# Row-paired transposes for the token-major rows and the attention output, and half 0's memory scores placed behind the third group of row pairs

## Chip, core and metric

The kernel runs on one NeuronCore of a Trainium2 chip. The metric is the device time of one launch in microseconds (us). The core's engines are named as the profile names them: PE is the matrix engine (PEld its weight loads), DVE the vector engine, ACT the scalar engine, POOL the GpSimd engine, SP the engine that issues most transfers.

## What is computed

Two layers are applied twice to x (2048 tokens of 448 elements, bf16): A, attention with a recurrent memory, and B, a gated feed-forward layer. Each takes the layer-normed x, and its result is added to x. The reference, cut to the parts that matter (H = 16 heads of 256, M = 8 memory rows, segments of 32 tokens, F = 1792):

```python
def _A_ref(x, mem0, Wq, Wk, Wv, Wo, seg_len):
    ...
    mask = (idx[:, None] < M) | (idx[:, None] >= idx[None, :])
    mem = mem0
    for s in range(n_seg):                      # 64 segments, one after another
        h = jnp.concatenate([mem, xs], axis=1)  # 8 memory rows and 32 tokens
        q, k, v = (einsum('btd,dhe->bhte', h, W) for W in (Wq, Wk, Wv))
        scores = jnp.einsum('bhqe,bhke->bhqk', q, k) * scale
        p = _softmax(jnp.where(mask, scores, -1e9))
        o = jnp.einsum('bhqk,bhke->bhqe', p, v)
        o = jnp.einsum('bhte,hed->btd', o, Wo)
        mem = o[:, :M, :]                       # the next segment's memory
        outs.append(o[:, M:, :])

def _B_ref(x, W_gate, W_up, W_down):
    gate = x @ W_gate
    h = gate * (gate > 0) * (x @ W_up)
    return h @ W_down

x = x + _A_ref(_layernorm(x), ...); x = x + _B_ref(_layernorm(x), ...)
x = x + _A_ref(_layernorm(x), ...); x = x + _B_ref(_layernorm(x), ...)
```

## The kernel before

**Weights are fused first.** A prologue builds, for each head, Wq Wk^T (`A_sb`, `A3`, `A3z`) and Wv Wo (`B_sb`). Attention then needs only h itself: queries are h times the fused matrix, keys and values are the rows h.

**Two chains in one step.** Layer A runs twice over the sequence, and the second run (chain 1) follows the first (chain 0) four segments later. `step(g, ff)` (lines 575 to 810) does segment g of chain 0 and segment g - 4 of chain 1 together; there are 69 steps, of which those with g from 4 to 63 have both chains. The 80 columns of a step are 40 rows of each chain. Every second step (odd g) also carries a `Feed` object `ff`: the feed-forward layer for a block of 64 tokens of each chain. These are called feed steps here, the others plain steps.

**The order on PE is written out by hand.** All matmuls and transposes go through `mm` and `tr` (lines 80 to 84), and `in_order` (lines 72 to 78) chains each to the one before. The order on DVE and ACT isn't fixed in this way: the framework that compiles the kernel orders their instructions by its own reckoning and adds all semaphores.

**PSUM banks.** A PSUM tile takes one bank. `ox` has a bank of its own (line 583); all other tiles, with the tag "ps", share seven (line 67). A new tile can be written only when a bank has been given up by all readers of an earlier tile.

**The part of a step around the change** (lines 734 to 754). The 56 query tiles of a step (28 for each half `hf` of the heads) are built in banks of up to six tiles (`Bank`, lines 464 to 475; tile name `prj`). The 448 rows of the contraction are 3 x 128 + 64. The last 64 are computed first, for two banks at a time, by 64-row matmuls that lie in the upper and in the lower half of the array (`open_banks`, lines 484 to 495: "row pairs"). `close_bank` (lines 497 to 522) then adds the three full 128-row parts, 18 matmuls a bank (12 for the banks with number 4), and copies the result out to `TQ` or `TZ` on DVE or ACT. There are three groups of row pairs in a step: banks b0 and b2; banks b1, b3, z0 and z1; banks c0, c2, c1 and c3. b and z0 are what half 0 needs, c and z1 belong to half 1.

Between these stand the steps that the change touches:

- `ff.residual()` (lines 395 to 400, feed steps): four 128x128 transposes turn the attention output `OT`, which is kept dimension-major, into the tile `otp`; one DVE addition adds it to `xa` (line 399), and `row_stats` (lines 153 to 162) starts the layer norm.
- `hk_make()` (lines 588 to 596): four 128x128 transposes of the rows h (`hT`, dimension-major, 128 token columns) into the tile `kps`. DVE copies 128x512 of it to `hk` (line 593), and ACT copies the last dimension block once more into two places (line 594). `hk` is used as keys' rows in `weigh_m` and `weigh_x` later in the step.
- `scores_m(0)` (lines 598 to 604): the memory rows' scores of half 0, four matmuls into the tile `Sm` that read `TQ[0]` and `TZ[0]`. Its softmax (`weights_of`, lines 527 to 547, tags `mx`, `se`, `ssum`, `rs`, `PM`) runs on DVE and ACT. `flipped(PM[0], ...)` (line 756) transposes the result, and `weigh_m(0, ...)` (line 758, tile `ya`) uses it as `PT`.
- `ff.norm()` (line 751): two DVE operations that write `xn` (lines 164 to 172). They are pinned behind what was traced on DVE before them, which is the last operation of the softmax of `scores_m(0)`.

A row-paired transpose exists in the kernel already, in `flipped_rows` (lines 557 to 568, tile `ppr`): each 64 rows of the input are transposed by a 64-row matmul against a 64x64 identity, and the upper and the lower one go to two tiles, thus two banks.

Of the kernel before, what the change touches and what calls it, by code (L numbers as in the profile page):

```python
# [8 lines left out]
BF = mybir.dt.bfloat16  # L9
# [3 lines left out]
ALU = mybir.AluOpType  # L13
AX = mybir.AxisListType

DM = 448
# [15 lines left out]
HI = 128  # L32
# [7 lines left out]
ROWS = (slice(0, 64), slice(64, 128))  # L40
# [12 lines left out]
def build_kernel(ctx, tc, A_x, A_mem0, A_Wq, A_Wk, A_Wv, A_Wo, B_W_gate, B_W_up, B_W_down, out,  # L53
                 ntiles=16, nseg=64):
    nc = tc.nc
    P = nc.NUM_PARTITIONS
# [10 lines left out]
    psum = ctx.enter_context(tc.tile_pool(name="psum", bufs=7, space=bass.MemoryType.PSUM))  # L67
# [4 lines left out]
    def in_order(r):  # L72
        if last_pe[0] is not None:
            tc.add_manual_dep(r.ins, last_pe[0],
                              mybir.DependencyInfo(mybir.DependencyClass.NoSync,
                                                   mybir.DependencyReason.DATA),
                              reason="order of issue")
        last_pe[0] = r.ins.name

    def mm(*a, **k):  # L80
        in_order(nc.tensor.matmul(*a, **k))  # L81

    def tr(*a):
        in_order(nc.tensor.transpose(*a))  # L84

    def evac(eng, dst, src):
        if eng is nc.scalar:
            nc.scalar.copy(dst, src)  # L88
        else:
            eng.tensor_copy(dst, src)  # L90
# [10 lines left out]
    ident = glob.tile([P, P], BF, name="ident")  # L101
# [46 lines left out]
    for hf in range(2):  # L148
        t = glob.tile([P, 5, 6, 64], BF, name=f"TQ{hf}")
        nc.gpsimd.memset(t[:], 0.0)  # L150
        TQ.append(t)

    def row_stats(t):

        stats = p_ln.tile([P, nc.vector.BN_STATS_DIM], F32, tag="ln_stats")
        nc.vector.bn_stats(stats[:], t[:])  # L156
        mv = p_ln.tile([P, 2], F32, tag="ln_mv")
        nc.vector.bn_aggr(mv[:], stats[:])
        rstd = p_ln.tile([P, 1], F32, tag="ln_rstd")
        nc.gpsimd.tensor_scalar(out=rstd[:], in0=mv[:, 1:2], scalar1=EPS, scalar2=None, op0=ALU.add)  # L160
        nc.gpsimd.tensor_tensor(out=rstd[:], in0=rstd[:], in1=half[:], op=ALU.pow)
        return t, mv, rstd
# [209 lines left out]
    OT = main.tile([P, 4, 128], BF, name="OT")  # L372
# [11 lines left out]
    class Feed:  # L384
# [8 lines left out]
            self.nx = xp[i % 2]  # L393

        def residual(self):
            tp = psum.tile([P, 4, 128], BF, tag="ps", name="otp")
            for kd in range(4):
                tr(tp[:, kd, :], OT[:, kd, :], ident[:])
            nc.vector.tensor_tensor(self.x[:], tp[:].rearrange("p k d -> p (k d)")[:, 0:DM], self.x[:], op=ALU.add)
            self.st = row_stats(self.x)  # L400

        def norm(self):
# [54 lines left out]
    def moving(hb, j, idx, chains, rows=slice(0, P)):  # L457

        if len(chains) == 2:
            return hb[rows, j, idx * HI:(idx + 1) * HI].rearrange("p (c k) -> p c k", k=64)[:, :, 0:L]  # L460
        c = chains[0]
        return hb[rows, j, idx * HI + 64 * c:idx * HI + 64 * c + L]
# [14 lines left out]
    def last_rows(hf, t):  # L477

        if t >= 24:
            return hf, A3z[ROWS[hf], t - 24, :]  # L480
        kd, eo, p4 = t // 8, t // 4 % 2, t % 4
        return eo, A3[ROWS[eo], hf, 4 * kd + p4, :]

    def open_banks(chains, hb, j, *which):

        n = L * len(chains)
        banks = [Bank(hf, i) for hf, i in which]
        for a, b in zip(banks[::2], banks[1::2]):
            for k in range(len(a.tiles)):
                for bk in (a, b):  # L490
                    t = bk.tiles[k]
                    r, w = last_rows(bk.hf, t)
                    mm(bk.out(t, n), w, moving(hb, j, 3, chains, ROWS[r]), start=(k == 0), stop=False,
                       skip_group_check=True)
        return banks

    def close_bank(bk, chains, hb, j, eng):

        n = L * len(chains)
        hf, N = bk.hf, len(bk.tiles)  # L500
        for t in bk.tiles:
            for kd in range(3):
                mm(bk.out(t, n), A_sb[:, kd, hf, t, :], moving(hb, j, kd, chains), start=False, stop=(kd == 2),
                   skip_group_check=True)
        ps = bk.ps
        if bk.i < 4:
            at = 2 * (bk.i // 2) + bk.i % 2
            parts = [(eng, slice(0, P), TQ[hf][:].rearrange("p g (k b) w -> p g k (b w)", b=2)[:, :, :, 32 * at:32 * at + 32], 3)]
        else:
            parts = [(nc.vector, slice(0, 64), TZ[hf][0:64, :, 0:64].unsqueeze(2), 1),  # L510
                     (nc.scalar, slice(64, 128), TZ[hf][64:128, :, 64:128].unsqueeze(2), 1)]
        for eng, rows, T, K in parts:
            T = T.rearrange("p g k (t q) -> p k t g q", q=16)
            if len(chains) == 2:
                evac(eng, T, ps[rows, 0:N * n].rearrange("p (k t g q) -> p k t g q", k=K, t=N // K, q=16))
                continue
            c = chains[0]
            src = ps[rows, 0:N * n].rearrange("p (k t w) -> p k t w", k=K, t=N // K)
            x, m = (0, SEG) if c == 0 else (MEM, 0)
            evac(eng, T[:, :, :, 2, MEM * c:MEM * c + MEM], src[:, :, :, m:m + MEM])  # L520
            evac(eng, T[:, :, :, 3 * c:3 * c + 2, :],
                 src[:, :, :, x:x + SEG].rearrange("p k t (g q) -> p k t g q", q=16))
# [47 lines left out]
    def active(g):  # L570
        return [c for c in (0, 1) if 0 <= g - c * LAG < nseg]
# [3 lines left out]
    def step(g, ff):  # L575
        chains = active(g)
        xs = active(g - 1)
        ms = [c for c in chains if g - c * LAG + 1 < nseg]
        gb, j = divmod(g, BLK)
        hb = hTb[gb % 2]  # L580
# [5 lines left out]
            return YY[hf][(g + later) % 2]  # L586

        def hk_make():
            kps = psum.tile([P, 4, 128], BF, tag="ps", name="kps")
            for i in range(4):  # L590
                tr(kps[:, i, :], hb[:, j, i * HI:(i + 1) * HI], ident[:])
            hk = HK[g % 2]
            nc.vector.tensor_copy(hk[:, 0:4, :], kps[:])
            nc.scalar.copy(hk[:].rearrange("p k n -> p (k n)")[:, 512:768].rearrange("p (a b) -> p a b", b=64)[:, 0::3, :],
                           kps[:, 3, :].rearrange("p (a b) -> p a b", b=64))
            return hk

        def scores_m(hf):
            if not ms:
                return  # L600
            Sp = psum.tile([P, 2, L], F32, tag="ps", name="Sm")
            for kd in range(4):
                mm(Sp[:, :, :], queries(hf, 2, kd), moving(hb, j, kd, (0, 1)), start=(kd == 0), stop=(kd == 3))
            weights_of(Sp, 2, PM[hf], blk[:], f"m{hf}")
# [135 lines left out]
        b1, b3, z0, z1 = open_banks(chains, hb, j, (0, 1), (0, 3), (0, 4), (1, 4))  # L740
        close_bank(z0, chains, hb, j, None)
        load_some()
        close_bank(b1, chains, hb, j, nc.vector)
        close_bank(b3, chains, hb, j, nc.scalar)
        hk = hk_make()
        close_bank(z1, chains, hb, j, None)
        scores_m(0)
        c0, c2, c1, c3 = open_banks(chains, hb, j, (1, 0), (1, 2), (1, 1), (1, 3))
        close_bank(c0, chains, hb, j, nc.scalar)
        if ff is not None:  # L750
            ff.norm()
# [66 lines left out]
    for g in range(nsteps + 1):  # L818
        if g == LAG - 1:
            set_mem(LAG, mem0T[:].unsqueeze(2), (1,))  # L820
        i = (g - 3) // 2
        step(g, Feed(i) if g % 2 and 0 <= i < nblk + LAG // BLK - 1 else None)
# [11 lines left out]
@with_exitstack  # L834
def kernel(
    ctx: ExitStack,
    tc: tile.TileContext,
    A_x: bass.AP,
    A_mem0: bass.AP,
    A_Wq: bass.AP,  # L840
    A_Wk: bass.AP,
    A_Wv: bass.AP,
    A_Wo: bass.AP,
    A_seg_len: bass.AP,
    B_x: bass.AP,
    B_W_gate: bass.AP,
    B_W_up: bass.AP,
    B_W_down: bass.AP,
    out: bass.AP,
):  # L850
    S = A_x.shape[1]
    ntiles = S // 128
    build_kernel(ctx, tc, A_x, A_mem0, A_Wq, A_Wk, A_Wv, A_Wo, B_W_gate, B_W_up, B_W_down, out,
                 ntiles=ntiles, nseg=4 * ntiles)
# [35 lines left out]
```

## Time and profile before

| | |
|---|---|
| time, median of 3 runs (lowest to highest) | 1609.27 us (1607.51 to 1610.35) |
| the profiled execution: its time; its span | 1606.34 us; 1604.6 us |
| granted PE clock, mean | 0.993 |
| busy: PE / PEld / DVE / ACT / POOL | 1577.4 / 1446.3 / 1142.0 / 771.1 / 70.5 us |
| `kps`: 272 transposes, 216 to 314 ns each; DVE copy x68; ACT copy x68 | median 219; 424; 265 ns |
| `otp`: 136 transposes; DVE addition x34 | median 219; 378 ns |
| `ppr`: 198 row-paired transposes; DVE copy x33; ACT copy x33 (128x192 each) | median 188 to 190; 257; 325 ns |
| `Sm` softmax: `mx`, `se`, `PM` on DVE, exp on ACT | 231, 235, 232; 265 ns |

A matmul's duration covers its way through the array. Several are under way at once, so a run of matmuls advances by the distance between their starts, which is far shorter than one duration; a wait shows as a larger distance, not as idle time. Times of the timeline are in us from the start of the span.

### The profile page before, as it was taken

The numbers are of one execution on the slowest core, as the hardware profiler recorded it, in microseconds if no ns is written. First come the engines' busy times: TensorE is split into PE (matmuls) and PEld (weight loads), VectorE is DVE, ScalarE is ACT, GpSimd is POOL, SyncE is SP. The second block draws the span as 40 slices with busy tenths as digits, with TensorE's granted clock in tenths as the row PEclk, the third lists the DMA queues.
The fourth block names the chain that finished last, engine by engine and source line by source line (L and its number), as shares of the span: only waits on it lengthen the run. The fifth ranks groups of instructions, "written<-read, shape, count | busy, mean of one in ns | idle before, by whom it ended". The sixth has DMA issues, their size and how long they took to land.

```text
span 1604.6 us, 96546 instructions
## 1 busy us (share of the span) xinstructions
PE 1577.4 (98%) x44476; PEld 1446.3 (90%) x44476; DVE 1142.0 (71%) x3859; ACT 771.1 (48%) x2239; POOL 70.5 (4%) x156
## 2 busy tenths in 40 slices
PE   9999999999999999999999999999999999999997
PEld 7688899999999999999999999999999999999886
DVE  7756777777777777777767777776777777777673
ACT  6644444554444444544444444544444444544442
POOL 2100000000000000000000000000000000000000
PEclk9989999999999999999999999999999999999999
DMA  9530000000000000000000000000000000000000
GB/s 257 160 87 9 8 10 9 4 10 9 10 10 10 10 10 8 6 10 10 9 10 10 10 10 5 8 10 10 10 10 9 10 10 5 9 8 7 7 7 6
DMA packets 29461, 33.02 MB, mean 21 GB/s; under 512 B 3320, under 2 KB 28160, under 8 KB 29056
## 3 DMA queue, kind: packets, MB, share of 16 engines
q1 hardware_dynamic: 28992, 26.85, 6.3%
q8 instruction: 347, 5.69, 1.5%
q14 instruction: 58, 0.48, 0.1%
q0 software_dynamic: 64, 0.01, 0.0%
HBM read 23.18 MB, written 1.84 MB: 16 GB/s over the span
## 4 chain that ended last, share of the span: by engine, by line
PE 86%; DVE 7%; ACT 5%; issue 1%; DMA 0%; SPq 0%; POOL 0%; POOLq 0%; ACTq 0%; DVEq 0%
PE ox L81 25%; PE prj L81 22%; PE ups L81 10%; PE dps L81 6%; PE o L81 5%; PE Sx L81 3%; PE y L81 3%; PE Sm L81 2%; ACT Z L88 1%; PE bps L81 1%; DVE TQ L90 1%; DVE stats L156 1%; PE tpw L84 1%; PE aps L81 1%; PE gps L81 1%
## 5 line engine op out<-in xcount | busy, mean ns | idle before, releaser
L81 PEld LDWEIGHTS <-B_sb 128*128 128x128 bf16 (+1 forms) x15456 | 494.9, 103 | 28.7 <-issue 20.8
L81 PE MATMUL prj<-hT,A_sb 128*128 128x80 bf16 (+1 forms) x11424 | 442.3, 200 | 0.6 <-issue 0.6
L81 PEld LDWEIGHTS <-A_sb 128*128 128x128 bf16 x11424 | 410.6, 100 | 13.2 <-issue 0.7
L88 ACT CAST TQ<-prj 128x480 bf16<-128x480 f32 (+1 forms) x380 | 184.0, 496 | 111.1 <-PE prj L81 82.5
L81 PE MATMUL ox<-Y,B_sb 128*128 128x80 bf16 (+4 forms) x5880 | 223.0, 198 | 2.1 <-DVE Y L625 1.9
L81 PE MATMUL ox<-Z,B_sb 128*128 128x80 bf16 (+2 forms) x5712 | 217.8, 199 | 1.4 <-DVE Z L625 1.3
L81 PE MATMUL ups<-xT,Wgu_sb 64*128 64x128 bf16 (+1 forms) x3332 | 191.1, 214 | 2.1 <-DVE hh L423 0.8
L81 PE MATMUL gps<-xT,Wgu_sb 64*128 64x128 bf16 (+1 forms) x3332 | 191.3, 214 | 1.2 <-issue 0.9
L81 PEld LDWEIGHTS <-Wgu_sb 64*128 64x128 bf16 x6664 | 179.4, 95 | 5.2 <-issue 3.1
L90 DVE CAST TQ<-prj 128x480 bf16<-128x480 f32 (+1 forms) x228 | 129.0, 574 | 36.9 <-PE prj L81 34.7
L423 DVE SCALAR_TENSOR_TENSOR hh<-gps,ut 128x256 bf16<-128x256 f32 (+1 forms) x238 | 94.4, 407 | 48.7 <-ACT ut L422 35.0
L422 ACT CAST ut<-ups 128x256 bf16<-128x256 f32 (+1 forms) x238 | 85.5, 359 | 82.8 <-PE gps L81 63.6
L88 ACT CAST Y<-y 64x128 bf16<-64x128 f32 (+2 forms) x256 | 89.3, 379 | 46.9 <-DVE Y L90 41.8
L90 DVE CAST Y<-y 64x128 bf16<-64x128 f32 (+2 forms) x256 | 102.0, 419 | 13.6 <-ACT Y L88 4.6
L90 DVE CAST Z<-y 64x128 bf16<-64x128 f32 (+2 forms) x256 | 99.2, 418 | 12.4 <-ACT Z L88 5.5
L88 ACT COPY hT<-tps 128x256 bf16<-128x256 bf16 x32 | 11.9, 372 | 195.2 <-DVE hT L90 195.2
L554 DVE COPY PT<-pps 128x128 bf16<-128x128 bf16 (+1 forms) x206 | 49.8, 255 | 78.2 <-PE pps L84 75.4
L88 ACT CAST TZ<-prj 64x320 bf16<-64x320 f32 (+2 forms) x152 | 56.0, 378 | 98.7 <-DVE TZ L90 92.7
L88 ACT CAST Z<-y 64x128 bf16<-64x128 f32 (+2 forms) x256 | 89.2, 378 | 24.1 <-DVE Z L90 17.4
L81 PEld LDWEIGHTS <-TQ 128*128 128x128 bf16 x1938 | 85.2, 97 | 13.6 <-ACT TQ L88 7.9
L542 DVE TENSOR_REDUCE ssum<-se 128x2 f32<-128x80 f32 (+1 forms) x270 | 70.8, 274 | 35.5 <-ACT se L536 33.3
L81 PE MATMUL dps<-Wd_sb,hh 128*128 128x448 bf16 x476 | 96.0, 353 | 0.0
(125 smaller groups left out, 2244.3 us busy)
## 6 DMA issues: line engine op xcount, KB each, us to landing
wo<-in_A_Wo_dram SPq DMA_DIRECT2D x8, 448.0 KB, 7.7
nat<-in_A_Wq_dram SPq DMA_DIRECT2D x8, 384.0 KB, 5.4
nat<-in_A_Wk_dram SPq DMA_DIRECT2D x8, 384.0 KB, 5.8
nat<-in_A_Wv_dram SPq DMA_DIRECT2D x8, 384.0 KB, 7.6
xa<-in_A_x_dram SPq DMA_DIRECT2D x32, 56.0 KB, 2.2
xa<-xp SPq DMA_DIRECT2D x32, 56.0 KB, 1.9
out_dram<-xa SPq DMA_DIRECT2D x32, 56.0 KB, 2.0
xp<-in_A_x_dram SPq DMA_DIRECT2D x30, 56.0 KB, 2.1
```

What stands on the lines that cost most here:

```text
L81: in_order(nc.tensor.matmul(*a, **k))
L84: in_order(nc.tensor.transpose(*a))
L88: nc.scalar.copy(dst, src)
L90: eng.tensor_copy(dst, src)
L156: nc.vector.bn_stats(stats[:], t[:])
L422: nc.scalar.copy(ut[:, :, n], ups[:, :, n])
L423: nc.vector.scalar_tensor_tensor(out=hh[:, 2 * u:2 * u + 2, n], in0=gps[:, :, n], scalar=0.0, in1=ut[:, :, n], op0=ALU.max, op1=ALU.mult)
L542: nc.vector.tensor_reduce(ssum[:], se[:], axis=AX.X, op=ALU.add)
L554: nc.vector.tensor_copy(PT[:], pps[:].rearrange("p b q -> p (b q)"))
```

## The change

The diff adds a helper, uses it for `otp` and `kps`, and moves two lines.

```diff
@@ -149,6 +149,14 @@
+    def flipped_dims(name, src):
+
+        two = [psum.tile([P, 4, 64], BF, tag="ps", name=name) for _ in range(2)]
+        for kd in range(4):
+            for r in range(2):
+                tr(two[r][:, kd, :], src(r, kd), ident[ROWS[r], ROWS[r]])
+        return two
@@ -393,10 +401,10 @@
         def residual(self):
-            tp = psum.tile([P, 4, 128], BF, tag="ps", name="otp")
-            for kd in range(4):
-                tr(tp[:, kd, :], OT[:, kd, :], ident[:])
-            nc.vector.tensor_tensor(self.x[:], tp[:].rearrange("p k d -> p (k d)")[:, 0:DM], self.x[:], op=ALU.add)
+            tp = flipped_dims("otp", lambda r, kd: OT[ROWS[r], kd, :])
+            xd = self.x[:].rearrange("p (c d) -> p c d", d=64)
+            for r in range(2):
+                nc.vector.tensor_tensor(xd[:, r::2, :], tp[r][:, 0:4 - r, :], xd[:, r::2, :], op=ALU.add)
             self.st = row_stats(self.x)
@@ -586,13 +594,12 @@
         def hk_make():
-            kps = psum.tile([P, 4, 128], BF, tag="ps", name="kps")
-            for i in range(4):
-                tr(kps[:, i, :], hb[:, j, i * HI:(i + 1) * HI], ident[:])
+            kps = flipped_dims("kps", lambda r, kd: hb[ROWS[r], j, kd * HI:kd * HI + HI])
             hk = HK[g % 2]
-            nc.vector.tensor_copy(hk[:, 0:4, :], kps[:])
+            for r, eng in enumerate((nc.vector, nc.scalar)):
+                evac(eng, hk[:, 0:4, 64 * r:64 * r + 64], kps[r][:])
             nc.scalar.copy(hk[:].rearrange("p k n -> p (k n)")[:, 512:768].rearrange("p (a b) -> p a b", b=64)[:, 0::3, :],
-                           kps[:, 3, :].rearrange("p (a b) -> p a b", b=64))
+                           kps[1][:, 3, :].unsqueeze(1).to_broadcast([P, 2, 64]))
             return hk
@@ -742,10 +749,10 @@
         load_some()
         close_bank(b1, chains, hb, j, nc.vector)
         close_bank(b3, chains, hb, j, nc.scalar)
+        close_bank(z1, chains, hb, j, None)
         hk = hk_make()
-        close_bank(z1, chains, hb, j, None)
+        c0, c2, c1, c3 = open_banks(chains, hb, j, (1, 0), (1, 2), (1, 1), (1, 3))
         scores_m(0)
-        c0, c2, c1, c3 = open_banks(chains, hb, j, (1, 0), (1, 2), (1, 1), (1, 3))
         close_bank(c0, chains, hb, j, nc.scalar)
```

Each set of four 128-row transposes becomes eight 64-row ones, in pairs, into two tiles instead of one. The addition of the attention output becomes two (128x256 and 128x192). The copy of `kps` is divided between DVE and ACT (128x256 each). On PE the order after bank b3 was: `kps`, bank z1's full part, `Sm`, the row pairs of the c banks, c0. It becomes: z1's full part, `kps`, the row pairs of the c banks, `Sm`, c0. The `otp` transposes stay where they were, directly ahead of the row pairs of b1, b3, z0 and z1.

## The prediction

> **What bounds the kernel now.** I read the page's first and fourth part first.
>
> ```profile
> PE 1577.4 (98%) x44476; PEld 1446.3 (90%) x44476; DVE 1142.0 (71%) x3859; ACT 771.1 (48%) x2239; POOL 70.5 (4%) x156
> ...
> PE 86%; DVE 7%; ACT 5%; issue 1%; DMA 0%; SPq 0%; POOL 0%; POOLq 0%; ACTq 0%; DVEq 0%
> ```
>
> PE sets the end, and no other engine is near its limit over the whole span. What counts is therefore each place where PE starts late. Next comes the timeline of PE around the change, in a feed step (start, duration, engine, line).
>
> ```profile
> 798.24 0.39 PE L84 MATMUL otp<-ident,OT 128*128 128x128 bf16 x4
> ...
> 798.56 0.39 PE L81 MATMUL prj<-hT,A 64*128 64x80 bf16 x12
> ...
> 798.78 0.31 PE L81 MATMUL prj<-hT,A3z 64*128 64x80 bf16 x8
> ...
> 799.02 1.89 PE L81 MATMUL prj<-hT,A_sb 128*128 128x80 bf16 x48
> ...
> 800.75 0.39 PE L84 MATMUL kps<-ident,hT 128*128 128x128 bf16 x4
> ...
> 800.98 0.59 PE L81 MATMUL prj<-hT,A_sb 128*128 128x80 bf16 x12
> ...
> 801.67 0.15 PEld L81 LDWEIGHTS <-TQ 128*128 128x128 bf16 x3 [0.23 <-ACT TQ L88]
> 801.67 0.28 PE L81 MATMUL Sm<-hT,TQ 128*128 128x80 bf16 x3
> ...
> 801.92 0.60 PE L81 MATMUL prj<-hT,A 64*128 64x80 bf16 x24
> ...
> 802.46 2.75 PE L81 MATMUL prj<-hT,A_sb 128*128 128x80 bf16 x72
> ```
>
> The reader should take distances between starts. `kps` to the next run is 0.226 us: 0.057 a transpose. Full 80-column matmuls are 0.036 apart (48 from 799.02 to 800.75). Row pairs also take 0.036 a pair. A change between full and 64-row matmuls costs 0.095 to 0.10 on top. The wait is at `Sm`: the twelfth matmul of bank z1 starts at 801.37 (0.59 less one duration of 0.20), `Sm` only at 801.67, 0.27 later than its turn. PEld names ACT's copy of bank b3 to `TQ`. In the plain step before, the same reckoning (12 from 782.47, `Sm` at 783.06) gives 0.16. Over 30 feed and 30 plain steps with both chains that is 12.9 us, the only recurring wait of PE that I find. The chain of waits over this stretch tells why b3's copy is late.
>
> ```profile
> 798.33 0.66 DVE TQ L90
> 798.98 0.31 DVE xa L399
> ...
> 799.31 0.64 DVE stats L156
> ...
> 800.16 0.38 DVE TZ L90
> ...
> 800.61 0.43 ACT TZ L88
> ...
> 801.06 0.57 ACT TQ L88
> ```
>
> DVE is full from 798.3 to 800.5, and its queue, not PE, leads to `Sm`. This matters below, because the first line, the copy of bank b0, also says when a bank comes free.
>
> **The transposes.** The trace has row-paired transposes of the same form in `flipped_rows`.
>
> ```profile
> 810.17 0.19 PE L84 MATMUL ppr<-ident,PM 64*128 64x64 bf16 x2
> ...
> 810.20 0.22 PE L84 MATMUL ppr<-ident,PX 64*128 64x64 bf16 x4
> ...
> 810.25 0.22 PE L81 MATMUL ups<-xT,Wgu_sb 64*128 64x128 bf16 x1
> ```
>
> Three pairs take 0.086 us, so four take 0.115 against 0.226: 0.11 saved in each `kps` and each `otp`. The number of changes between full and 64-row work stays the same in every step (in before the row pairs, out after), so nothing is gained or lost there.
>
> **The wait at `Sm`** for b3's copy ends: z1, `kps` and the c pairs now lie between. Taken alone, a feed step would gain 0.11 + 0.11 + 0.27 and a plain step 0.11 + 0.16.
>
> **What the second bank costs.** Seven banks serve all tiles but `ox`. `otp` and `kps` now take two each, and I count what is live at each opening.
>
> *At z1, feed step.* Ahead of z1 come four tiles of the previous step's `weigh_x(1)`, then b0, b2, otp, otp, b1, b3, z0. One bank is free at the start, four come back from `weigh_x(1)`, so with the second otp z1 is the first that must wait for b0, b2 or otp. The earliest is b0, copied on DVE until 798.98. An ACT copy's end is followed by PE 0.05 later (801.62 to 801.67), so z1 opens at 799.04. PE would be there at 798.67 (0.11 earlier than 798.78): 0.37 of waiting, the full matmuls start at 799.28, 0.26 later than before. Sixty of them (z0, b1, b3, z1) at 0.0357 end at 801.42, the change of mode gives `kps` at 801.52, the c pairs 801.64, and `Sm`'s turn is 802.17.
>
> *At `Sm`, every step.* Live are z1, two kps, c0, c2, c1, c3: all seven. The c banks are closed only after `Sm`, so `Sm` must wait until z1 or one kps is copied out. DVE copies z1 first (ready 0.24 after its last matmul as in all these rows, 0.48 long: 801.63 to 802.11), then the first kps. That copy, 128x256, is priced by this row, 0.29:
>
> ```profile
> L554 DVE COPY PT<-pps 128x256 bf16<-128x256 bf16 x103 | 29.6, 287 | 73.8 <-PE pps L84 73.8
> ```
>
> Independent DVE operations overlap by 0.08, so it ends at 802.32 and `Sm` starts at 802.38, 0.21 late. Four matmuls later, without a change of mode, c0 starts at 802.53; it was 802.46. **Feed step: 0.07 lost.** Plain step by the same sum: z1 782.24, `kps` 782.77, turn of `Sm` 783.42, z1's copy 782.88 to 783.36, kps copy until 783.57, `Sm` 783.63, c0 783.78 against 783.85: **0.06 gained.**
>
> The Trainium skill, "TensorEngine Tiling (Array Packing)", section "Gotcha 1: PSUM Pressure", says that different row tiles have to write to different banks and so raise the demand for banks. By that rule the sum is the one here; if one bank could hold both, it would be the gain of the paragraph before. The trace agrees as far as it goes: `ppr` holds its two halves in two tiles.
>
> **What the later `Sm` pushes.** `Sm` now stands directly ahead of c0, so its softmax has 0.64 less time. PE's transpose of it still finds it ready (0.5 to spare). DVE in feed steps does not:
>
> ```profile
> 803.61 0.24 DVE L547 TENSOR_TENSOR PM<-se,rs 128x80 bf16<-128x80 f32 x1
> 803.77 0.60 DVE L170 TENSOR_SCALAR xn<-xa,mv,rstd 128x448 bf16<-128x448 bf16 x2
> 804.61 0.66 DVE L90 CAST TQ<-prj 128x480 bf16<-128x480 f32 x1 [0.24 <-PE prj L81]
> ...
> 805.31 0.22 DVE L554 COPY PT<-pps 128x128 bf16<-128x128 bf16 x1
> ...
> 805.58 0.27 PE L81 MATMUL ya<-PT,hk 128*128 128x128 bf16 x2
> ```
>
> `PM` moves with `Sm` (2.12 to 2.18 after its start) to 804.53; `xn` is pinned behind it and ends at 805.05; the copy of c1 follows until 805.63 and `PT` until 805.78, where before it waited only for PE. `ya` then starts at 805.83 instead of 805.65: **0.17 lost in a feed step.** Bounds: nothing if DVE takes `PT` first, 0.3 if ACT's exp is late too. In a plain step there is no `xn`, and c1's copy ends in time.
>
> **Other engines.** The addition (380 ns for 448 columns; 0.535 ns a column from the copies of 256 and 512) becomes 277 + 243: 0.14 more, at most 0.38 if each half took the whole. It delays `stats` and b1's copy, which has 0.35 until DVE's next ready work (z1 at 801.63): 0. ACT gets a 128x256 copy, about 0.37 (its `hT` copies take 372 ns); it sits idle 0.3 to 0.5 around each, and exp starts no later. If that cover goes, ACT delays the `Sm` softmax, which has 0.5. Transfers: none added, and none on SP or POOL is moved past.
>
> **Sum.** 30 feed steps x (0.07 + 0.17) = 7.2; 30 plain steps x 0.06 = 1.8 gained; the eight steps with one chain and the last feed-forward pass: 12 sets of transposes x 0.11 = 1.3 gained, against shorter single-chain work that waits more for the same banks; I take 0. Net +5.4: the profiled execution's 1606.3 (its span of 1604.6 and 1.7 around it) would be 1611.7. It lies 2.9 below the median of the runs, so I state **1614.7 us**.
>
> **Rivals.**
>
> - *`Sm` is given another bank.* The framework decides at compile time which bank `Sm` takes. The second kps (ACT: 0.37 + 0.27 after it is ready) is free some 0.17 later than the first, z1 (ACT copies after DVE) 0.24 later. x 60: 10.4 to 14.5 on top, **1625 to 1629**. For it: the two releases are within 0.2 us by my sum, and the order is reckoned, not measured. Against: by the sum above the first kps is the earliest.
> - *DVE copies kps ahead of z1* (the faster side). Then the first kps is free 0.24 after the transposes plus 0.29, almost at `Sm`'s turn: c0 is 0.25 earlier in a plain step, 0.11 in a feed step, `ya` still loses 0.17. 30 x (0.25 - 0.06) = 5.7 gained: **1603.6**. It decides as soon as the kps copy starts before z1's. For it: before, `hk` did precede z1 on DVE. Against: z1 now ends 0.22 before kps is ready, and DVE is free then.
> - *`ya` doesn't wait* (`PT` ahead of c1's copy): 30 x (0.07 - 0.06) = +0.3, **1609.6**. Against: c1 is ready first.
> - *No bank wait at all, the change does what it does on PE*: 30 x 0.76 = 22.8, **1586.5**. Against: seven banks and the count above.
>
> **Numbers.** Chances: my forecast 0.45, another bank 0.20, kps first 0.17, no `ya` wait 0.14, no bank wait 0.04. A measurement of this kernel tells 0.2% (3.2 us) from no change. Faster: 0.17 + 0.04 and 0.02 from the edges, 0.23. Same: 0.12 of the third rival and 0.05 of my own, 0.17. Slower: 0.60. My forecast alone spans 1611 to 1620 (bounds of `ya` and the bank of z1, which costs 2 us more if it is b2's); the range to the other cases is 1601 to 1629.
>
> **What would show it.** In the profile after: z1's first row pair follows b0's copy by 0.05 in feed steps; `Sm` follows a `hk` copy, not `TQ`; `kps` to the next run is 0.115; `ya` follows `PT`, and `PT` follows c1's copy. If `Sm` starts one mode change after the last c pair, the bank count is wrong, and with it the sign.

## The result and the profile after

The changed kernel takes 1613.0 us (median of 6 runs, 1612.73 to 1614.5) against 1609.0 of the kernel before (6 runs, 1605.95 to 1610.54): 1.0026 times the time before, 95% interval 1.0014 to 1.0037. It is 4 us slower (2.3 to 6.0 by the interval); 5.4 were forecast. The profiled execution took 1613.1 us, its span is 1611.0. The page's busy times and its chain, by engine:

```profile
PE 1573.4 (98%) x44884; PEld 1444.9 (90%) x44884; DVE 1135.0 (70%) x3893; ACT 788.3 (49%) x2307; POOL 70.5 (4%) x156
...
PE 87%; DVE 7%; ACT 3%; issue 1%; DMA 0%; SPq 0%; POOL 0%; POOLq 0%; ACTq 0%; DVEq 0%
```

Between the two profiled executions, PE is busy 4 us less and the span is 6.4 us longer. The work on PE shrank and its waits grew, so the totals can't show where; the timeline of a feed step does (start, duration, engine, line, and in brackets the idle time and what ended it).

```profile
801.15 0.66 DVE L90 CAST TQ<-prj 128x480 bf16<-128x480 f32 x1
...
801.16 0.29 PE L84 MATMUL otp<-ident,OT 64*128 64x64 bf16 x8
...
801.29 0.38 PE L81 MATMUL prj<-hT,A 64*128 64x80 bf16 x12
...
801.50 0.20 PE L81 MATMUL prj<-hT,A3z 64*128 64x80 bf16 x1
...
801.87 0.30 PE L81 MATMUL prj<-hT,A3z 64*128 64x80 bf16 x7 [0.17 <-DVE TQ L90]
...
802.10 2.32 PE L81 MATMUL prj<-hT,A_sb 128*128 128x80 bf16 x60
...
804.35 0.29 PE L84 MATMUL kps<-ident,hT 64*128 64x64 bf16 x8
...
804.46 0.48 DVE L90 CAST TZ<-prj 64x320 bf16<-64x320 f32 x1 [0.42 <-PE prj L81]
...
804.48 0.59 PE L81 MATMUL prj<-hT,A 64*128 64x80 bf16 x24
...
804.87 0.27 DVE L90 COPY hk<-kps 128x256 bf16<-128x256 bf16 x1
...
805.19 0.27 PE L81 MATMUL Sm<-hT,TQ 128*128 128x80 bf16 x3
```

Three readings. The eight `A3z` matmuls, which before were one group, are split: z0's first starts at 801.50, z1's only at 801.87, 0.06 after DVE's copy of bank b0 ended (801.15 + 0.66). The eight `kps` matmuls take 0.13 until the next work, where four full ones took 0.23. And `Sm` starts at 805.19: the last c pair starts at 804.87 (0.59 less one duration of 0.20), one change of mode (0.13 from start to start) later is 805.00, so 0.18 is waiting, and what ends just before is DVE's copy of the first half of `kps` (804.87 + 0.27 = 805.14), not the copy to `TQ` of the kernel before. The chain of waits over this stretch says the same in five lines.

```profile
801.15 0.67 DVE TQ L90
...
801.87 2.57 PE prj L81 x67
...
804.46 0.48 DVE TZ L90
804.94 0.21 DVE hk L90
...
805.19 0.30 PE Sm L81 x4
```

Further on in the same step, the softmax of `Sm`, the layer norm and the copies behind it on DVE:

```profile
807.11 0.24 DVE L555 TENSOR_TENSOR PM<-se,rs 128x80 bf16<-128x80 f32 x1
807.27 0.60 DVE L178 TENSOR_SCALAR xn<-xa,mv,rstd 128x448 bf16<-128x448 bf16 x2
807.78 0.65 DVE L90 CAST TQ<-prj 128x480 bf16<-128x480 f32 x1
...
808.35 0.21 DVE L562 COPY PT<-pps 128x128 bf16<-128x128 bf16 x1
...
808.41 0.18 PE L81 MATMUL Sx<-hT,TZ 128*128 128x40 bf16 x1
...
808.62 0.27 PE L81 MATMUL ya<-PT,hk 128*128 128x128 bf16 x2
```

The four DVE groups stand without a gap, and `ya` starts 0.06 after `PT`'s copy: DVE's queue holds PE here. `ya` starts 0.20 after the start of the last `Sx` matmul (808.41), where in the kernel before it started 0.03 after it; so 0.17 is waiting.

The length of a step, taken from one step's first row pair (b0 and b2) to the next one's, makes all kernels of this study comparable; a step differs by less than 0.01 us from one to the next in the middle of the run. Medians over the middle steps, in us, with the measured time as a ratio to the kernel before, run on the same chip:

| kernel | feed step | plain step | ratio (95% interval) |
|---|---|---|---|
| before | 27.04 | 18.29 | 1 |
| the change | 27.24 | 18.18 | 1.0026 (1.0014 to 1.0037) |
| e1: otp in one bank | 27.00 | 18.18 | 0.9979 (0.9970 to 0.9989) |
| e2: kps in one bank | 27.18 | 18.12 | 0.9995 (0.9985 to 1.0004) |
| e3: only the order | 26.93 | 18.12 | 0.9955 (0.9942 to 0.9969) |
| e4: the change, norm early | 27.07 | 18.18 | 0.9992 (0.9982 to 1.0002) |
| e5: only the transposes | 27.23 | 18.29 | 1.0033 (1.0020 to 1.0045) |
| e6: the change, kps copied first | 27.07 | 18.01 | 0.9966 (0.9954 to 0.9977) |
| e7: only the order, norm early | 26.76 | 18.12 | 0.9915 (0.9901 to 0.9929) |
| e8: all that gained | 26.72 | 18.01 | 0.9893 (0.9879 to 0.9907) |
| e9: e1 with two additions | 27.00 | 18.18 | 0.9973 (0.9962 to 0.9983) |
| e10: before, norm early | 27.04 | 18.29 | 0.9997 (0.9985 to 1.0009) |

### The profile page after: what moved, and what is told of

Same layout as the page of the kernel before. It is cut to its first block, busy times and chain, and to the rows that moved or that the text cites. A ratio compares the mean times of both kernels' runs of the same rounds, so it can differ in the third digit from the quotient of the medians.

```text
span 1611.0 us, 97401 instructions
## 1 busy us (share of the span) xinstructions
PE 1573.4 (98%) x44884; PEld 1444.9 (90%) x44884; DVE 1135.0 (70%) x3893; ACT 788.3 (49%) x2307; POOL 70.5 (4%) x156
## 4 chain that ended last, share of the span: by engine, by line
PE 87%; DVE 7%; ACT 3%; issue 1%; DMA 0%; SPq 0%; POOL 0%; POOLq 0%; ACTq 0%; DVEq 0%
PE ox L81 25%; PE prj L81 24%; PE ups L81 10%; PE dps L81 6%; PE o L81 5%; PE Sx L81 4%; PE y L81 3%; PE Sm L81 2%; DVE TZ L90 2%; ACT Z L88 1%; PE bps L81 1%; DVE TQ L90 1%; PE pps L84 1%; PE aps L81 1%; PE tpw L84 1%
## 5 line engine op out<-in xcount | busy, mean ns | idle before, releaser
L81 PE MATMUL prj<-hT,A_sb 128*128 128x80 bf16 (+1 forms) x11424 | 430.6, 200 | 0.6 <-issue 0.4
L81 PEld LDWEIGHTS <-A_sb 128*128 128x128 bf16 x11424 | 406.0, 100 | 9.2 <-issue 0.8
L544 ACT ACTIVATE se<-se 128x80 f32<-128x80 f32 (+1 forms) x270 | 71.4, 298 | 63.4 <-DVE se L543 62.6
L81 PEld LDWEIGHTS <-TQ 128*128 128x128 bf16 x1938 | 90.0, 96 | 12.2 <-ACT TQ L88 0.5
```

The lines of the kernel that those rows point to most:

```text
L544: nc.scalar.activation(se[:], se[:], AF.Exp, scale=SCALE)
```

## The experiments

The theory: the second bank of each row-paired transpose makes PE wait for a bank, at z1 and at `Sm`, and the later `Sm` pushes DVE's queue into `ya`. The rivals: the later softmax is the whole loss; or the extra evacuation work is.

**e1, the attention output in one bank.** The change with `residual` as it was:

```diff
-            tp = flipped_dims("otp", lambda r, kd: OT[ROWS[r], kd, :])
-            ...
+            tp = psum.tile([P, 4, 128], BF, tag="ps", name="otp")
+            for kd in range(4):
+                tr(tp[:, kd, :], OT[:, kd, :], ident[:])
+            nc.vector.tensor_tensor(self.x[:], tp[:].rearrange("p k d -> p (k d)")[:, 0:DM], self.x[:], op=ALU.add)
```

> The changed kernel with the attention output turned by four full transposes into one bank and one addition, as before; kps and the order stay changed. Theory (banks): z1's opening no longer waits for b0's copy (0.33 us in a feed step), the full transposes cost 0.11 more, so a feed step is 0.22 shorter than in the changed kernel and a plain step the same: 1613.0 - 30 x 0.22 = 1606.4 us. Rival (the later softmax of half 0's memory scores is the whole loss): otp has nothing to do with it, and its transposes are 0.11 longer: 1613 to 1616 us. Rival (more evacuation work on DVE and ACT): one addition instead of two saves 0.14 us of DVE in a feed step, at most 4 us: 1609 us.

Measured 1604.49 us against 1607.75, ratio 0.9979: a feed step is 0.25 shorter than in the change (0.22 expected), a plain step the same. The timeline of the feed step in e1, at the same place:

```profile
799.32 0.66 DVE L90 CAST TQ<-prj 128x480 bf16<-128x480 f32 x1
...
799.77 0.31 PE L81 MATMUL prj<-hT,A3z 64*128 64x80 bf16 x8
...
800.01 2.32 PE L81 MATMUL prj<-hT,A_sb 128*128 128x80 bf16 x60
```

The eight `A3z` are one group again and run while b0 is still being copied (until 799.98). The bank count was right, and the longer transposes are far cheaper than the wait.

**e2, the token-major rows in one bank.** The change with `hk_make` as it was, in the new order:

```diff
-            kps = flipped_dims("kps", lambda r, kd: hb[ROWS[r], j, kd * HI:kd * HI + HI])
+            kps = psum.tile([P, 4, 128], BF, tag="ps", name="kps")
+            for i in range(4):
+                tr(kps[:, i, :], hb[:, j, i * HI:(i + 1) * HI], ident[:])
```

> The changed kernel with kps turned by four full transposes into one bank and copied as before; otp and the order stay changed. Theory (banks): six of seven banks are live at Sm, so its wait for the first half's copy (0.18 us in every step) goes; the full transposes put Sm's turn 0.10 later; net 0.085 shorter in 60 steps: 1613.0 - 5.1 = 1607.9 us, and Sm follows the last c pair by one mode change. Rival (later softmax): nothing gained, 0.10 longer in 60 steps: 1619 us. Rival (evacuation work): DVE copies 128x512 again, 0.14 us more a step, ACT less: 1613 us or more.

Measured 1607.18 us against 1607.75, ratio 0.9995; both kinds of step are 0.06 to 0.07 shorter than in the change (0.085 expected).

```profile
799.81 0.60 PE L81 MATMUL prj<-hT,A 64*128 64x80 bf16 x24
...
800.35 0.28 PE L81 MATMUL Sm<-hT,TQ 128*128 128x80 bf16 x3
```

In this trace `Sm` follows the last c pair by the change of mode alone: 0.095 beyond the row pair's own distance in the median of all steps, where the change has 0.28. Transposes at nearly twice the price (0.226 against 0.126 us) are the faster ones here.

**e3, only the order.** Both edits of e1 and e2, so that against the kernel before only this is left:

```diff
+        close_bank(z1, chains, hb, j, None)
         hk = hk_make()
-        close_bank(z1, chains, hb, j, None)
-        scores_m(0)
         c0, c2, c1, c3 = open_banks(chains, hb, j, (1, 0), (1, 2), (1, 1), (1, 3))
+        scores_m(0)
```

> Only the order is changed (z1's full part, kps, the c pairs, then half 0's memory scores); both sets of transposes are as before, one bank each. Theory (banks): both gains of the two kernels above add up: 1613.0 - 6.6 - 5.1 = 1601.3 us; against the kernel before this is the wait at Sm gone (0.27 feed, 0.16 plain), the wait at ya of 0.17 in feed steps kept: 1609.0 - 30 x 0.43 + 30 x 0.17 = 1601.2 us, the same from the other side. Rival (later softmax): the move is the loss, so 1609 us or slower, up to 1614.

Measured 1600.99 us against 1607.75, ratio 0.9955. The move by itself is a gain of 7 us, so the later softmax isn't the loss of the change as a whole; what it does cost, the wait at `ya`, is still in this kernel and is taken out in e7.

**e4, the layer norm ahead of the scores.**

```diff
         c0, c2, c1, c3 = open_banks(chains, hb, j, (1, 0), (1, 2), (1, 1), (1, 3))
+        if ff is not None:
+            ff.norm()
         scores_m(0)
         close_bank(c0, chains, hb, j, nc.scalar)
-        if ff is not None:
-            ff.norm()
```

> The changed kernel with the layer norm's two DVE operations (xn) called ahead of half 0's memory scores instead of behind c0, so that they stand ahead of the softmax on DVE. Theory: ya's wait for PT (0.18 us in a feed step) goes, the two bank waits stay (z1 0.33, Sm 0.18): 1613.0 - 30 x 0.18 = 1607.7 us. Rival (later softmax is the whole loss, and DVE's queue its way to PE): the loss of 4 us goes entirely and with it the gain of the shorter transposes shows: 1601 us or less. Rival (xn in front delays the softmax so that its transpose becomes late): 1613 us or slower.

Measured 1605.59 us against 1607.75, ratio 0.9992; a feed step is 0.17 shorter than in the change, a plain step the same. DVE in e4:

```profile
802.41 0.59 DVE L178 TENSOR_SCALAR xn<-xa,mv,rstd 128x448 bf16<-128x448 bf16 x2
...
804.48 0.24 DVE L555 TENSOR_TENSOR PM<-se,rs 128x80 bf16<-128x80 f32 x1
...
804.82 0.66 DVE L90 CAST TQ<-prj 128x480 bf16<-128x480 f32 x1
...
805.51 0.23 DVE L562 COPY PT<-pps 128x128 bf16<-128x128 bf16 x1
...
805.79 0.27 PE L81 MATMUL ya<-PT,hk 128*128 128x128 bf16 x2
```

`xn` fills time in which DVE had nothing else ready, the copy of c1 no longer queues behind it, and PE's trace has no wait at `ya` left (0.03 after the last `Sx` matmul, as in the kernel before). The other two waits stay, as expected.

**e5, only the transposes.** The change with the order of the kernel before:

```diff
-        close_bank(z1, chains, hb, j, None)
         hk = hk_make()
-        c0, c2, c1, c3 = open_banks(chains, hb, j, (1, 0), (1, 2), (1, 1), (1, 3))
+        close_bank(z1, chains, hb, j, None)
         scores_m(0)
+        c0, c2, c1, c3 = open_banks(chains, hb, j, (1, 0), (1, 2), (1, 1), (1, 3))
```

> Only the transposes are changed (both row-paired, two banks each); the order is that of the kernel before, so kps stands between two full-row parts (b3 and z1) and half 0's memory scores ahead of the c pairs. Theory (banks and changes of mode): z1 still waits for b0's copy in feed steps (0.26 later after the shorter otp), kps is 0.11 shorter but takes two more changes of mode (0.20); both are partly swallowed by the wait of Sm for b3's copy, which stays (0.16 plain, 0.27 feed). Plain step: 0; feed step: Sm is bound by DVE's queue, which has 0.14 more work in the two additions, so +0.14: 1609.0 + 30 x 0.14 = 1613 us. Rival (the shorter transposes are a gain, and the later scores the loss): 102 x 0.11 gained, 1598 us.

Measured 1614.52 us against 1608.65, ratio 1.0033: the feed step 0.19 longer than before (0.14 expected), the plain step unchanged to 0.001. So the paired transposes alone lose as much as the whole change. In a feed step z1 waits as in the change:

```profile
803.53 0.20 PE L81 MATMUL prj<-hT,A3z 64*128 64x80 bf16 x1
...
803.89 0.30 PE L81 MATMUL prj<-hT,A3z 64*128 64x80 bf16 x7 [0.16 <-DVE TQ L90]
...
806.11 0.56 ACT L88 CAST TQ<-prj 128x480 bf16<-128x480 f32 x1 [0.15 <-PE prj L81]
...
806.72 0.28 PE L81 MATMUL Sm<-hT,TQ 128*128 128x80 bf16 x3
```

The expected 0.14 came near, but not by the way it was worked out. It was to come from DVE's queue with its two additions; here ACT's copy of b3 waits for PE (the third line), so it is PE's lateness after the wait at z1 that reaches `Sm`. In a plain step `Sm` starts 0.85 after b3's last matmul, in this kernel and in the one before: that is the time until b3's copy is done. `kps` stands behind that matmul, so its two more changes of mode fall into a wait that was there already.

**e6, kps copied ahead of z1.** `close_bank` is divided into its matmuls (`close_sums`) and its copies (`close_copies`); the copies of z1 are emitted and pinned behind those of `kps`. The edit in `step`:

```diff
-        close_bank(z1, chains, hb, j, None)
+        close_sums(z1, chains, hb, j)
         hk = hk_make()
+        close_copies(z1, chains, None, tc.keep_in_program_order)
```

> The changed kernel with one difference: the copies of bank z1 are emitted and pinned behind the copies of kps on DVE and ACT, so that the first half of kps gives up its bank first. Theory (banks): Sm's wait shrinks from 0.18 to 0.03 in 60 steps, z1's wait (0.33) and ya's (0.18) in feed steps stay: 1613.0 - 60 x 0.15 = 1604 us. Rival (Sm waits for the queries of half 0, not for a bank): no change, 1613 us.

Measured 1604.22 us against 1608.65, ratio 0.9966. Both kinds of step are 0.17 shorter than in the change. The feed step of e6:

```profile
799.61 0.29 PE L84 MATMUL kps<-ident,hT 64*128 64x64 bf16 x8
...
799.94 0.29 DVE L89 COPY hk<-kps 128x256 bf16<-128x256 bf16 x1 [0.64 <-PE kps L84]
...
800.14 0.47 DVE L89 CAST TZ<-prj 64x320 bf16<-64x320 f32 x1
...
800.28 0.27 PE L81 MATMUL Sm<-hT,TQ 128*128 128x80 bf16 x3
```

`Sm` again follows the end of the `hk` copy (800.23) by 0.05, while z1's copy has just begun. No work was removed, and `Sm` doesn't read `hk`; the copies of z1 were only put behind those of `kps`. This is what shows that `Sm` waits for a bank, and for whose.

**e7, only the order, norm early** (e3 with the edit of e4).

> The order changed alone (transposes as before, one bank each) and the layer norm's two DVE operations ahead of half 0's memory scores. Theory: the two gains add, since the waits are at different places: 7 us less than before from the order and 30 x 0.18 from ya: 1609.0 - 7.8 - 5.4 = 1595.8 us, with no wait at z1, Sm or ya. Rival (PE then meets another late engine): 1601 us as with the order alone.

Measured 1596.0 us against 1608.65, ratio 0.9915. The two gains add: the feed step is 0.17 shorter than in e3, the plain step the same, and none of the three waits is left.

**e8, all that gained.** `otp` in one bank (the edit of e1), `kps` paired and copied ahead of z1 (the edit of e6), the new order, and the norm one place earlier than in e4:

```diff
+        if ff is not None:
+            ff.norm()
         close_sums(z1, chains, hb, j)
         hk = hk_make()
         close_copies(z1, chains, None, tc.keep_in_program_order)
         ...
         close_bank(c0, chains, hb, j, nc.scalar)
-        if ff is not None:
-            ff.norm()
```

> Everything that gave something: otp in one bank as before, kps row-paired with its copies pinned ahead of z1's, the order changed, the layer norm's DVE operations ahead of z1's full part. Theory: against the kernel above kps is 0.10 shorter in 60 steps, less 0.02 of waiting at Sm: 1595.8 - 60 x 0.085 = 1590.7 us. Rival (a wait for the bank at Sm is left, since xn now stands on DVE ahead of the copy of kps in feed steps): up to 0.3 lost in 30 feed steps, 1600 us.

Measured 1591.97 us against 1608.65 (4 runs, 1590.27 to 1594.86), ratio 0.9893: the fastest kernel of the study, 1.1% below the kernel before. Against e7, `kps` paired is worth 0.10 in a plain step, and 0.04 in a feed step together with the norm's new place: there `xn` keeps DVE busy until the `kps` copy can start, 0.40 after the first transpose where e6 has 0.33, and 0.03 of waiting is left at `Sm`. The chain of e8, by engine:

```profile
PE 95%; DVE 2%; ACT 1%; issue 1%; DMA 0%; POOL 0%; SPq 0%; POOLq 0%; ACTq 0%; DVEq 0%
```

PE's share of the chain, 86% before and 87% after the change, is 95%: little of the chain is left to waits for another engine. The share is a rough sign only, since e3 has 96% with the wait at `ya` still in it.

**e9, the two additions without the second bank** (e1, its addition divided as in the change).

```diff
-            nc.vector.tensor_tensor(self.x[:], tp[:].rearrange("p k d -> p (k d)")[:, 0:DM], self.x[:], op=ALU.add)
+            xd = self.x[:].rearrange("p (c d) -> p c d", d=64)
+            for r in range(2):
+                nc.vector.tensor_tensor(xd[:, r::2, :], tp[:].rearrange("p k (r d) -> p k r d", d=64)[:, 0:4 - r, r, :],
+                                        xd[:, r::2, :], op=ALU.add)
```

> The kernel e1 (otp by four full transposes into one bank, the rest as in the change), with its one addition on DVE divided into the change's two of 128x256 and 128x192, so that only DVE's extra work of otp is put back, not the second bank. Theory: DVE has room for the 0.14 us in a feed step before its next work is ready, so no change against e1: 0.998 of the kernel before (at most 0.5 us off). Rival (the extra evacuation work is what otp's pairing costs): 30 x 0.14 to 30 x 0.25, 1.0005 to 1.002 of the kernel before.

Ratio 0.9973 (1604.94 us against 1610.46), e1 had 0.9979; feed steps are equal to 0.001. DVE's extra work in `residual` costs nothing in this order, so what e1 gained over the change is the bank.

**e10, the kernel before with the norm early.** In the order before, `ff.norm()` stands directly ahead of `scores_m(0)`:

```diff
         close_bank(z1, chains, hb, j, None)
+        if ff is not None:
+            ff.norm()
         scores_m(0)
         ...
         close_bank(c0, chains, hb, j, nc.scalar)
-        if ff is not None:
-            ff.norm()
```

> The kernel before with the layer norm's two DVE operations ahead of half 0's memory scores, nothing else. Theory (ya's wait comes only with the later scores): the kernel before has no wait at ya to remove, so no change, 0.999 to 1.001. Rival (DVE's queue in feed steps costs PE in the kernel before too): up to 5 us gained, 0.997.

Ratio 0.9997, steps unchanged. `ya`'s wait is not in the kernel before; the move brings it.

## Why the prediction was right

- **What bounds.** Right: PE's waits decide, and the one that the prediction names in the kernel before, at `Sm`, is gone in e3. Its cause was told too simply ("its queue, not PE"). `Sm` starts 0.96 after b3's last matmul in a feed step and 0.85 in a plain step, so DVE's queue adds 0.11 in feed steps; the rest of the wait is b3's copy itself, behind PE's own work. The forecast doesn't rest on this, as the move takes away the whole wait.
- **The transposes.** Four pairs take 0.126 instead of the forecast 0.115: 0.10 saved each. None of it reaches the end, as forecast: behind `otp` it goes into the wait at z1 and behind `kps` into the wait at `Sm`, and with the full transposes back the steps are shorter (e1, e2).
- **z1's wait.** Forecast 0.37, found 0.36 (801.50 to 801.87), ended by b0's copy as named. Removing it gave 0.25 net of the longer transposes (e1); the prediction's own net is 0.26. The expectation of e1 had taken the wait as 0.33, and so 0.22 net.
- **`Sm`'s wait.** Forecast 0.21, found 0.18, for the first half of `kps`, as chosen among three banks. The half copy takes 0.273, not 0.29. The rival *kps first* priced its removal: 1603.6 forecast, 0.9966 x 1609.0 = 1603.5 in e6. That the framework would not choose this order was right.
- **`ya`'s wait.** Forecast 0.17, found 0.17. Without it 1609.6 was forecast, and e4's ratio on 1609.0 is 1607.7.
- **Other engines at nothing.** Right for the additions (e9). On ACT the order came out otherwise than I had it, the second half of `kps` ahead of z1's copy, which cost nothing since neither frees the first bank.
- **The sum.** Feed step +0.24 forecast, +0.21 found; plain step -0.06 forecast, -0.10 found. With unrounded medians that is 3.1 us over 30 steps of each kind, where 5.4 was forecast: the waits were right one by one, and their small errors add up over 60 steps. The measured 4.0 us, with an interval of 2.3 to 6.0, can't tell the two apart, so that it lies near the forecast is in part luck. The two profiled executions differ by 6.4 us of span: about 2.5 in the stretch with both chains (its first feed step is 0.5 shorter after the change), 2.1 ahead of it and 1.9 behind it, which I had set at 0. These two parts also differ without a cause in the change: e10, whose steps are as long as before, has a span 4.3 us longer than the kernel before, nearly all of it there. So how much of them the change causes is open.
- **A second bank as such.** That both halves of a pair need two banks, the rule of the Trainium skill ("TensorEngine Tiling (Array Packing)", section "Gotcha 1: PSUM Pressure"), was not tried by putting both into one. What the runs show is its price: with one bank less in use at the opening of z1 (e1) and of `Sm` (e2) the wait is gone.

The mechanism came out as it was told, wait by wait: each of the three waits was within 0.03 us of the forecast, and e1, e4 and e6 each take out the one they aim at (e6 all but 0.02). The size of the total is less sure than this, as said above.

## What to carry to other kernels

An edit that makes PE's work shorter but holds one more PSUM bank has to be judged at the next opening: list which banks are in use there, and see which copy frees a bank first and when its engine gets to it. A wait that ends with a copy on another engine swallows every saving on PE between the work that the copy reads and the wait. The paired `kps` cost 4 to 5 us in the change (e2: 0.06 a step, or the difference of the ratios) and gained 4 (e7 to e8) once its copies went ahead of another bank's. When a step is moved later, look for what is pinned behind its results on another engine; here two unrelated operations held the queue.

## What was not expected of the hardware

The changes between full and 64-row matmuls cost 0.093 to 0.098 us each in every kernel here, whether full matmuls, transposes or score matmuls stood on the other side. A longer wait takes the change of mode in: in the changed kernel PE starts 0.05 after the end of the copy that frees its bank at `Sm`, where a change of mode lies between, and 0.06 after it at z1, where none does. With unchanged work, steps repeat to within 0.01 us, so a difference of 0.05 us in a step could be read from a single profile where the measured times of whole runs scatter by 5 us.
